# One recorded order for another: the second half of a planned fused kernel (long convolution and gated MLP, forward and backward)

## The chip, the cores and the metric

The kernel runs on one NeuronCore of a Trainium2 chip. Five instruction streams work side by side: TensorE (PE: matmuls, with PEld for its weight loads), VectorE (DVE), ScalarE (ACT), GpSimd (POOL) and SyncE (SP), which here issues all DMAs. Sixteen DMA engines move data between HBM and SBUF. Matmuls write to PSUM, eight banks of 2 KB a partition, which ACT and DVE empty. The metric is device microseconds of one launch, the median of several runs.

## What is computed

With `x = A_q` (2048 x 512) and `xn = layernorm(x)`, the output is `x + A(xn) + B(xn)`. A is a short convolution of `k` (four taps), times `v`, then a convolution over the whole sequence by FFT, plus `kv * D`, times `xn`. B is a gated product of matmuls. The program returns the output and the gradients with respect to all nine inputs:

```python
def _A_ref(q, k, v, shift_k, ssm_k, ssm_D):
    ...
    kv = k_shift * v
    ...
    y_f = kv_f * kf_f[None, :, :, :]
    y = irfft2(y_f, ...)[:, 0, :S, :]
    y = y + kv * ssm_D[None, None, :]
    return q * y
def _B_ref(x, w_gate, w_up, w_down):
    g = einsum("bsd,df->bsf", x, w_gate); u = einsum("bsd,df->bsf", x, w_up)
    return einsum("bsf,fd->bsd", g * u, w_down)
x = A_q; xn = _layernorm(x, axis=-1)
return x + _A_ref(xn, ...) + _B_ref(xn, ...)
```

## The kernel before

**How an order is set.** The program text does not fix the order of the instructions. Every call on an engine goes through the class `Eng` (L145), which only records an `Op`; matmuls that follow one another into the same PSUM slot are joined into one operation of at most 2200 columns. At the end `emit` (L181) unpacks the string `PLAN`: a list of 2271 operation numbers, and a PSUM bank for each of 398 slots. The operations are then issued in that order, so `PLAN` decides the order on PE (1009 operations), DVE (623), ACT (377), POOL (3) and SP (259 DMAs) and which buffer of PSUM each result uses. Waits between engines follow from the data: an instruction waits for what it reads, and for the readers of what it overwrites. All instructions have the line of the recording helper, L173, in the profile.

**Stages.** The first 100 us hold the loads, the layernorm, the first F steps and the short convolution (`a_gen`). The feature axis F = 1376 is cut into six F steps j. `mlp_rows(j, r)` (L417) computes for two of the sixteen row blocks the down-projected gradient `pd` and the two products `pg`, copies them out of PSUM and multiplies them; the result goes to a ring in SBUF and, through `hd_store`, to the scratch tensor HD in HBM. `dw_gen(j)` (L584) makes the weight gradients of F step j: chains of sixteen 512-wide matmuls.

The spectral stage (`s_gen`, some 125 to 257 us) takes eight pairs of slabs from scratch AX: `s_B` and `s_Bi` are packed small matmuls (tiles of 64x32 and 32x64 of the array, sixteen to an operation) with copies by ACT behind them, `s_pw` the products on DVE; the result goes to scratch CX. The stages overlap: PE alternates between `mlp_rows`, `dw_gen` and the spectral operations.

The last stage (from 268 us) runs over n = 0..7, two row blocks each:

- `c_load(n)` (L678) loads 1.5 MB of CX into the single buffer `f["C"]`; `last_dft(n)` (L721) turns it by 24 packed matmuls into three PSUM results. They are copied by ACT and used on DVE by `c_dkv`, `c_y` and `c_o5`. The next `c_load` may start only when `last_dft` has read the buffer.
- `c_dsk(n)` (L766) multiplies rows of dks by rows of k on DVE and sums them by eight packed matmuls on PE. When its products are made, `k_load(n+1)` (L693) may overwrite the rows of k. `dk_pair` (L712) is seven DVE operations and a store.
- `hd_load(n)` (L644) brings HD back transposed by DMA, into one of two buffers. `y_o(n, rr)` (L786) and `y_x(n, rr)` (L803) read it: 11 and 22 matmuls of 512 columns. `y_o` ends in an addition and a store of the output, `y_x` in a chain of DVE and ACT operations (the layernorm gradient) and a store. `y_load(n)` brings the rows of x that `c_y(n)` needs, `dkv_load(n)` two operands of `c_dkv(n)`.
- `turn_gen` (L617) transposes ring blocks of the last F steps, by DMA for some and by PE for others.

All DMAs go through SP in the recorded order. An instruction that waits on SP holds up every DMA behind it.

Of the kernel before, what the change touches and what calls it, by code (L numbers as in the profile page):

```python
# [26 lines left out]
WO = [12 * sum(SW[:j]) for j in range(NST)]  # L27
# [11 lines left out]
def kernel(  # L39
# [223 lines left out]
    XT = rT.tile("XT", [128, 16, 1024])  # L263
# [62 lines left out]
    for i in range(12):  # L326
        w = 4 if i < 4 else 2
# [254 lines left out]
    f = {}  # L582
# [251 lines left out]
    F0, F1 = 240.0, 415.0  # L834
    O0, OJ = 230.0, 10.0
# [60 lines left out]
    A = Gen(a_all())  # L896
# [42 lines left out]
    for n in range(NCH):  # L939
        last = n + 1 == NCH  # L940
        t = F0 + n * DF
# [30 lines left out]
        else:  # L972
# [115 lines left out]
```

## Time and profile before

| What | Value |
|---|---|
| Median of 3 runs | 427.74 us (427.58 to 427.88) |
| The profiled execution | 426.57 us |
| Its span, first to last instruction | 424.4 us |
| Time around the span | 2.17 us |
| PE, DVE, ACT busy | 415.1, 349.0, 261.5 us |
| Granted TensorE clock | 0.998 |
| Matmuls / DMA issues | 3290 / 259 |
| DMA moved | 127.27 MB, mean 300 GB/s |

The "busy" of PE says that a matmul was in the array; waits shorter than a matmul do not show in it. In the row of the DMA engines a digit is the mean busy share of sixteen engines in one of 40 slices of 10.6 us; in a table by stretches the same share can exceed 1, because packets that queue in an engine overlap.

### The profile page before, as it was taken

What the parts mean: (1) busy time and instruction counts of PE and PEld (TensorE: products, weight loads), DVE (VectorE), ACT (ScalarE), POOL (GpSimd) and SP (SyncE); (2) the same over time, 40 slices, a digit from 0 to 9 for tenths busy, and PEclk for the clock granted to TensorE, in tenths of its full rate; (3) what the DMA queues carried; (4) which work ended last, traced back from release to release, by engine and by line L of the source; (5) the groups of instructions that cost most, each with busy time, mean ns of one, the idle gap of its engine ahead of it and who ended that gap; (6) DMA issues with size and microseconds to landing.
All of it is one profiled execution on the core that took longest, in us unless ns stands there. A gap on an engine that the chain in (4) does not pass through costs nothing.

```text
span 424.4 us, 8338 instructions
## 1 busy us (share of the span) xinstructions
PE 415.1 (98%) x3290; PEld 209.3 (49%) x3290; DVE 349.0 (82%) x653; ACT 261.5 (62%) x380; POOL 3.5 (1%) x9
## 2 busy tenths in 40 slices
PE   8999999999999999999999999999999899999995
PEld 5755555855675444544444344445444344444443
DVE  5999977998649989899999990325858799999996
ACT  4855988598644999888999953362525331323324
POOL 1000000000000000000000000000000000000000
PEclk9999999999999999999999999999999999999999
DMA  7989999999788869968878899999999999999964
GB/s 262 398 197 379 320 306 388 349 367 365 288 310 287 319 229 352 313 227 318 319 274 344 292 312 325 298 348 274 231 275 329 303 269 329 308 302 286 267 193 144
DMA packets 104366, 127.27 MB, mean 300 GB/s; under 512 B 63876, under 2 KB 74249, under 8 KB 103304
## 3 DMA queue, kind: packets, MB, share of 16 engines
q1 hardware_dynamic: 104328, 126.75, 93.5%
q8 instruction: 25, 0.41, 0.4%
q14 instruction: 13, 0.11, 0.1%
HBM read 57.10 MB, written 54.04 MB: 262 GB/s over the span
## 4 chain that ended last, share of the span: by engine, by line
PE 77%; DMA 10%; DVE 10%; issue 1%; SPq 1%; ACTq 0%; ACT 0%
PE PP L173 77%; DVE big L173 10%; DMA out_dram<-big 4%; DMA big<-CX 2%; DMA big<-in_k_dram 2%; SPq L173 1%; DMA big<-in_w_dram 1%; DMA big<-in_go_dram 1%; ACTq L1084 0%; ACT big L173 0%
## 5 line engine op out<-in xcount | busy, mean ns | idle before, releaser
L173 PE MATMUL PP<-big 128*128 128x512 bf16 (+8 forms) x3290 | 415.1, 345 | 4.3 <-DMA big<-CX 2.1
L173 PEld LDWEIGHTS <-big 128*128 128x128 bf16 (+4 forms) x3290 | 209.3, 97 | 209.7 <-issue 61.0
L173 DVE TENSOR_TENSOR big<-big 128x1024 bf16<-128x1024 bf16 (+2 forms) x465 | 267.7, 631 | 45.5 <-ACT big L173 36.6
L173 ACT CAST big<-PP 128x512 bf16<-128x512 f32 (+2 forms) x314 | 224.4, 780 | 82.1 <-PE PP L173 71.1
L173 ACT ACTIVATE big<-big 128x1 f32<-128x1 f32 (+3 forms) x46 | 23.6, 522 | 53.4 <-DVE big L173 50.5
L173 DVE CAST big<-PP 128x512 bf16<-128x512 f32 (+1 forms) x37 | 32.4, 875 | 9.8 <-PE PP L173 5.2
L173 ACT COPY big<-PP 128x1024 bf16<-128x1024 bf16 x15 | 14.9, 1010 | 18.3 <-PE PP L173 18.3
L173 DVE SCALAR_TENSOR_TENSOR big<-big 128x512 bf16<-128x512 f32 (+2 forms) x36 | 23.3, 654 | 0.2
L173 DVE SCALAR_TENSOR_TENSOR big<-big,PP 128x512 f32<-128x512 bf16 x14 | 9.6, 684 | 9.2 <-PE PP L173 9.2
L173 DVE BATCH_NORM_STATS2 big<-big 128x6 f32<-128x512 bf16 x16 | 10.6, 682 | 4.0 <-DMA big<-in_x_dram 3.9
L173 DVE TENSOR_TENSOR big<-big,PP 128x512 bf16<-128x512 bf16 x14 | 9.2, 683 | 1.5 <-PE PP L173 1.5
L173 POOL MEMSET big<- 128x1536 bf16 (+2 forms) x3 | 2.9, 950 | 252.4 <-PE PP L173 252.4
L173 DVE TENSOR_SCALAR big<-big 128x512 bf16<-128x512 bf16 (+1 forms) x13 | 4.6, 385 | 0.0
L173 ACT ACTIVATE big<-PP 128x512 f32<-128x512 f32 x2 | 1.2, 597 | 4.5 <-PE PP L173 4.5
L173 DVE BATCH_NORM_AGGREGATE big<-big 128x2 f32<-128x6 f32 x16 | 2.3, 169 | 0.1
L173 ACT ACT_TABLE_LOAD x1 | 1.3, 1283 | 0.7 <-PEq L1076 0.7
L173 DVE RECIPROCAL big<-big 128x2 f32<-128x2 f32 (+1 forms) x9 | 1.2, 151 | 0.6 <-ACT big L173 0.6
L173 DVE DVE_READ_ACCUMULATOR big<-big 128x1 f32 x16 | 1.3, 82 | 0.0
L173 DVE DVE_READ_ACCUMULATOR big<-big,PP 128x1 f32 x14 | 1.2, 82 | 0.0
L173 DVE MEMSET big<- 128x128 bf16 (+1 forms) x2 | 0.2, 112 | 0.8 <-PEq L1076 0.8
L173 DVE COPY big<-PP 128x1024 bf16<-128x1024 bf16 x1 | 0.7, 692 | 0.2 <-PE PP L173 0.2
L173 ACT ACTIVATION_READ_ACCUMULATOR big<-PP 128x1 f32 x2 | 0.4, 194 | 0.0
(6 smaller groups left out, 0.9 us busy)
## 6 DMA issues: line engine op xcount, KB each, us to landing
HD<-big SPq DMA_DIRECT2D x32, 384.0 KB, 5.4
AX<-big SPq DMA_DIRECT2D x16, 768.0 KB, 5.6
big<-AX SPq DMA_DIRECT2D x16, 768.0 KB, 6.0
CX<-big SPq DMA_DIRECT2D x16, 768.0 KB, 5.4
out_dram<-big SPq DMA_DIRECT2D x43, 256.0 KB, 3.8
big<-CX SPq DMA_DIRECT2D x7, 1536.0 KB, 8.0
big<-in_vK_dram SPq DMA_DIRECT2D x8, 512.0 KB, 5.1
big<-in_w_dram SPq DMA_DIRECT2D x4, 768.0 KB, 7.5
```

Of the source, the lines that this page charges most:

```text
L173: o.fns.append(lambda: f(*[fix(x) for x in a], **{kk: fix(x) for kk, x in k.items()}))
```

## The change

Two things are edited. In `mlp_rows`, the matmuls of `pg` are cut into two halves of 256 columns for fewer row blocks of F step 4: those with r < 4 instead of r < 8 (that is, r = 4 and r = 6: two halves of the row pair, four matmuls each, so 16 matmuls of 512 columns take the place of 32 of 256 columns).

And `PLAN` is another string. It unpacks to the same 2271 operations, in another order from operation 1100 on, and to another bank for 145 of the 398 slots. Up to there both orders are the same. On PE the first difference is at operation 517 of 1009, which starts at 170.12 us in the trace; on SP it is DMA 112 of 259, on ACT operation 201, on DVE operation 278. POOL's order is unchanged.

```diff
-PLAN = "c-l=@V-RM$vTb+9wr$(CZQHhO+qP}nHjZbGjlseDX6~O?yDOD...
+PLAN = "c-kdb1JowD5-nH8wr$(CZQHhO+qP}nHr6w1b7t|rf8I$t-IcDJ...
...
         for rr in range(2):
             pg = rN()[:, 0:2 * fw]
-            for p in (slice(0, fw), slice(fw, 2 * fw)) if j == 3 or j == 4 and r < 8 else (slice(0, 2 * fw),):
+            for p in (slice(0, fw), slice(fw, 2 * fw)) if j == 3 or j == 4 and r < 4 else (slice(0, 2 * fw),):
                 for c in range(4):
                     MM(pg[:, p], lhsT=xnT[:, r // 2, rr, c, :], rhs=wgu(j)[:, c, p], start=(c == 0), stop=(c == 3))
```

What differs in the unpacked order of the last stage, in the places that the prediction speaks of:

- On PE `c_dsk(n)` stands directly behind a `last_dft` for n = 0 to 4 and 6, and directly ahead of one for n = 5; before, three of the eight adjoined a `last_dft`. `last_dft(4)` stands later among the other matmuls, `last_dft(5)`, `(6)` and `(7)` earlier. The last `y_x` is `y_x(7, 0)` instead of `y_x(7, 1)`, and `c_dsk(7)` stands ahead of most of the last row pair's matmuls. The last operations of PE are `y_o(7, 1)` in both.
- On SP, from the middle of the stage on: `k_load(6)`, one of `dkv_load(6)`'s two transfers and the store of `dk_pair` of rows 6 and 7 stand ahead of `c_load(6)`, the store of `y_o(4)` behind it; `k_load(4)`, `dkv_load(4)` and `y_load(3)` stand ahead of `c_load(4)`; `hd_load(1)` stands ahead of `c_load(2)`; the DMA transpose of rows 8 and 9 stands ahead of `hd_load(0)` instead of behind `hd_load(4)`; `k_load(7)` stands ahead of `hd_load(7)` and `y_load(7)` behind it. The last DMA is the store of `y_o(7, 1)` instead of that of `y_x(7, 1)`.
- On DVE the last operation is the same one, the final addition of `y_x(7, 0)`; the chain of `y_x(7, 1)` ends some operations earlier.

More of the change, by code (lines that the diff above doesn't have):

```diff
@@ L33 @@
 EPS = 1e-5
-PLAN = "c-l=@V-RM$vTb+9wr$(CZQHhO+qP}nHjZbGjlseDX6~O?yDOD+8f*2gN+$rBAPF#(fE17tia`Pp$O0uHJ|u>OfRG%DgMxuWfG7|ZqCqK$4l$rKB!iex7GgmnC<E=GBb0;K5C?KWTqq9}AQfzcc#s?BLmt=!9iS6*hSZQB3P1~J1q&c4<b^a)5V}BX$O?s^Fyw==&<(mn5vUDap&1l~me3sPLJz0|J)s^{gP|}3>O&Q%4h^6xq=QB<3}!-Os03|bB8-R1Fc=!b5U2s;pb7MXiZBg^!w9GehhaLLfmN^zn!+g910!JqtcFQ28g@fl=m%+GFZ6~LkQ2thEXaacaUbl5*{~9hz&%Keec&u4!Glm8lVS~=3v*x|B*O!62(n>KTm$`KE%b$2m>qwD$*>OA!(tc!@8w5W0s~<KEQCd{6*j{y*aqq09Q+JR;TOmNTOcD`fIlHRE`#mxE1ZWZa1nOEamWTI;67Y}9C#FdgKO{zj=^I{jwc}no`RJ4JLJU6kP2@@YWxGPgWwPFDWt))cmp25O-P4#AwA~8444rgLMFTe&ml8p#+Q&AKZ8%8Hs(RaylD6WvctdN2pF&q)<wj8*beGpeS8D?F$xyIg4h86f`<4X6vC_UITXgI*a#crTX+gZunDfirnnwA;6{80EpQY54K1-1w#GL2B{akL&=z;XHjIIzaST3zub>@9!_C+pJ79DC0y<($+=7Sk2#&{C*a<sh7wn1?up7p~qsUkbzJ^zD4F8sIpgWGm*Dx7lV-6UH|G;+ai9PT;_!g$(G@OXXaSryv>DU{$VjrA~eQ^rTz<xLh7vK(Dh%@m7?!=SWA7|kJ9EiJd5I&_LG#FRlE*ye!aUL$ip|}#4;4mDHOK~U-f-_hY=i>-`2Fr06Er(V#664`2T#T!+H7&x^*pL!pF>FM|u`wmU_}GT(({NggO{gukpk}lO8_+52OiigJoy9Ix0%y{BEQuGe6qd%0R0hvsCmKQRs4QN>L|6{5;B_Rtfj6-{UdF3f0dL`LtcbJm4vwTzbQde(LaL1SunJbii`bm*V>Nt$4{<NXqyzW}ALA2zim|9YjlyR*i(*q8ic8ONHod@?c!}cCC-^DOp+mSIKf}-Q3ye<*=u1pUiD)i;h4ZK%rJ~%FhX&I=OigL%6(*+FScdvjTDpd1X+C|8-(We)OYfuujiJkwkIGYiszAM{0DX(!;rDn2l2AHIPZcQxRidQy1OA9(DI;Z~EA$f<q@OV}C8I)=g|bp*`UQW*-!L2fj(^~vn4Jn!4*Cm|QxU2{Z}2L;#iEpx-eGSVP1ookzQ@1uA5202;(u6-ic?i8K|n}EOw~weDy%^zBd6+=k^<GB1yqxwP)W)~QK=L~qpnnoYEx;7PW9+IEv9aCgX&NZ>O)ItDQ%=>)R(%`INC(xX$Nhi0W^W0(L~x#18FTyqUW@e*3%1GN0aF#ZJ=GWg{IInnnAbdFm0x(bdXNN5!z3m&~(~Ohv-MzLkH+6t)QRi811EB=_akD-{>N(rd70@ex_gO6nzh8=u<jPpVI^SozBu4Izf-=5eff6pV31)NlzjqmD6#0X8wXQa7KPbnK(0lMPE`Deoa~VFWO4C=^mY<H<XRD^Le^MIruK+<oA?||EApR{55?`d3Y#)L-*-B%FDptQ(Q)l$1yk`8^5Jt{Emk6Z2p%<@Jx=z|H?l!lK+v4Jc?s-d>+lwISP;A0z923aRQFYGk5~W;@Dh?EAuR#!xOm*CuGxtT!<(0IIhY;_mL~;cuvHLIr58i3Mb*hT#bLA|D*^PW!9;@gsbx+D#l5<F2x{G)kPddlkrkc&e1gmN7Ds-oQiV^F3C|frY_{g97E%1O0L22v@^%mQk+UtacVBj@imRs<XT*YV`*$nt!cO{m*YW{mJ?_~EzfDSHdo-pnobjGQq9kGxC<xIx?GRbYjUm688o9d;AGmByK#3;p*^@E_v9R!NgHuv&Z)gPrN-fc+Jt*^Q*Or1IhPWQ<=onWS8-ll&Re-9XVzt$N2}^Q-p19m6&KRE+?xAv8*a<1xi44OteRc>aZz2#*>oLe(KVc3*YjHL&xN(N=F<UOMC<4)e$6Gc9hcJfTuh5=N!`wM^=sb2WweIY(w<aPOKUkTuLHRQ-{%KhLCfkxe#C>gfIjAm+L51dC2g#Oxt><hr`(B~>N9@MFZdg7qA$6!w$TRqEpOmYxRHL!ZS^y5sGsu}+)kV6cl;%{(DvF%zvmygzW&HRaR*HzNo5)j(B|4vlSvo-nOkXcNg>^IkfxN*x{*`KK<%o%beMM6;W|QhacW5;`?$BJl>@w=hj2RSslV`G{gn@Ldg-e}w59Ih-#CK|)xA7YH}hfcp<B3*j?)R6OAc`k>8BZ`zmC`Gno}}KYn`aM<#*03lXZsf<ZO~%vPd5JgNw<ZJV|G3aapbBc&+A@3v`|@@I}7FYxFXY)+<~}uJRZSGDm0WpEOT5@k|}7bM-g}E-ec*iY(HovQAI%NuICkb(C(<XtG30$TeP}8+D3K)#!4HOUg36&Nn!QEYwxHMHlNCjwze;CYP01vRpUoVZFsG^*`FCw|NCG)uZ|sALSi-hmY}H-mY(Wn#PtrT1F1(J>IKt`84m-IFe6l$Puk2NBE@Xmzr`~Ys*fJD`$C^7Lwz-TMI}$Iibh&l-|+0a#jmUe0j%(C4t=2gi=%z$!?y{@41>Jmb-dJZ)$bfuYdC`J+BA#A3mVv<hEYZfBA+!(CfNYi^yd?r{(3U{>K-zl3daXQdzF(Lj|cQt>lr`k&F7dKGtS}(psMA7y4B1Yjb&~Rpl#fAq}LFRFRhQT))xJw2d^B#`01>)z|t+UT9nSM8DH7^`88okt0t2)W`Bh>&Ywqihq;8^u9chuT|tHeJJ0m%3J+i-fMm7CQap?ey=9&#HE8gl^?Z<{H?#~ulhtfN>=$t|JC315A81hX%FcnU&+t<hy0?Q1?-iy7qXu6g+w>BUSjs8M6=%F)<ybAUx{hYBpBN#qV`<kT36{O{UwHpy^#18$D-P&62;QmOBo>X>`!?u=`6kdB?D!U43@8Dh{Up?lFEijY)fDX?Tn<cq&8E|$~j47=Owjeu*8<!F33emVi|3gT#{rqTjoe6OKG1;X1gp`<cZCd6n0hSNq);>SuL9twE2?V7RWVODA#3?<g~@|spYf6mcw${PjW*(m!g*23RoW7EqQH;d?&-@sTH@9_JfR&$97Y0Nf8?<OJ$k-EVt#2?2)oo%nI3ZSs|tEM=4>e<c^fF=Qc`8Svf0jqh+<Ml<%dgjgh@l%_`bwwomp;bsH;dWUW-N19DK-$$F__8)T!@vT-tAzL7&x(~jE&*(B}kk$o!@WwTVW$~H+ROM9ClRjh+em1(j?I$B*jEJx(1)V5C6*``Y!>tZwHSLtf?Y>_Rt7q(Tl$#yv=FYRCJX2)fRbhlrmht;=d*3%l;2{|dfY>73rowC##*<0Bqr=+npv59tCnp$t`W6i9&^|cn((pp(RYi-MHxwWxL*49?oN}Ft-+Z6l4?#fhKWz*~jn{G4gOZ&w(+bipD1MGL(Vq5J;8)&O-jcv2vY>*AMwKmg+*eM%o+ijf<v-LL1X4?)MZgcFM&9$HH6Wd@TY^Tk$UAEhPvajs5?Xi(I-!|HLTVQ+bJKJab?GGDe2W+%0wC`<<owi?XtR1v*_Qp2Zc>Bf<*#vuQhwW=SVre|Bzq5ZVsRvKz#r=kfzqcr^9^IpQ3@2yL=q21drkC_sp4cy0H2>SqSZvSaH!Y6;Y3`Tptflt?9@jH_7BA>WEvv_K^dg?bvw3BY?^mpp|7G_qyXW*Ae!*J%Rjcl$y@uEH6rR${cml8G-&%gZZ*9DT=kktT$dmbhmces-VXy6-ysUTjw%*w5_(e<T<vfo!^+cZ6>v}$~=f%9dSMVlY(W`iBPwqv%i+A;DUdh|}bnoUfyoY!9ncm*3c|UL9{e76H@&P`}C;0=b>cf46gD>)CKG;|KIv?oce5BX+hThYA`6?gfOT4c)@*&>a*ZX*1?R~ttKeTIh%SQVcZ{@dbwr}t`KEdaC3!m$2e4~%`iN47<`%B;ALw&Nh^sRo~rubez>Yw;N-{znCVxQ`t`9VM8U-(-8(&zgH-|jp7fgkgw{*|Bc1^&uk`xRg2gZ#Lk@T-2-_xLee=#TuQpYs*I+`smnzS~dvE`RKYe7|4w)BcU0_rw0JU-zee!*6;B$-^zb?ce)Ff8n1;9_4rZ7k}m{0){Bzu15`*JX*NyDZ>+|5Iwx{w;m&W=kGjCxaU9kb59jG#0<aseUBA>^t9nOfA6Wo0gn^@_H^N)OZd~%huGmK&k+9cpFMF%7@CBCJyEC_a)$r>ch?X%WDH3{(~vCu<$rj*U?EqCA1Z~)!9%7{C{zi}Lgr94WC_(m$<REM3Ry$-P%xAZ*+PxbGL#90L++406bX4ktxz<y3S~q7&^ny3HlbKZ8rp`MAwjrfcddA65b}l`p<HMe+J_QhY-kb2h1y|gC?D#F0-;+NABKeqp+o2%`h||6VW<%5guY>7=oI>gNnv<s6efqdp>tRtMuZ+=N*E9}gq~qzSQWa2O<`ad8K#9kVNjSI28XF(b(kK8gi&F0*b+`!y)ZY74qL;*uqG@Bjl=eEEo=*2!=A7x91MrT;;<tu3HieHurwSFN5Y)2EZhh?!_hD%EDy)R%y2%e4L8H_a4XCUy~2qwEA$Sx!@004TnKl<j4(g!4ZFj>a5p>)7sJVLDLfDN!u_y6tP3l`<M1H72$#c?a4I|v2f~%GGMo-C!^3bjoC#;cqkv|pk=r_O<Z{g7C?MvMmL(jS7^^#*3%ikg5EBw0LWhVa0DI()>Ks{q)JG&Tm`CEFF}X#ef7B4c2X}}(qzn<9IO2>(5k;hdM!ZZSw{uZeG=&chJhF^r2ZhKXf*MJu5i=&khzeaGVr`MGjSzukpcZkCOd?t^6puK65I4n0`2T$op^q6qfHe9@=mVXPq$~n4V)SwRXh0C51poj0p!?r$1oKC}_A!h{>Id{8Ghn2Q5#%2zMW98tKGe!17~}(H{!pO^mB>mWmHQARQlm(uh_ipFsQw?pe}w%"
@@ new lines @@
+PLAN = "c-kdb1JowD5-nH8wr$(CZQHhO+qP}nHr6w1b7t|rf8I$t-IcDJLZ2=GWPxPBPzq8(YA6ATKp-2GhJ=t55(7d?C<zJ%4gsP;bcg|EAST3uvXBB|LwSe;NuV5bgw9X_;zB&g1M#6ERDv|H84^HVSP1!G3v_}m&=t}`K_~>Rpbad7<d7fIL1E|yZ6P}pfuc|V#zPP23B{l;bcYsD99lz5s1LoM9`uF=Py>d;ENBSTpe8he>W~4NzzCQPO`!_3gUK)vs=`oc48x!nOn_$42P(r17zv}GHXMbSa1PeM9%v3@U>}TzNw5~Cz*yJ|?O_0<hyBnORzYqU2Xi1BX2%0?5az;aI0g?ODfWZ&kPHt)O-zopa6Zg~1&{&{!4b%TwQ(H`g!RxL>R?X%0j9zR*a%Bu5WJV~VHpgDO|Tf2z;@UQcVGu(gbVN^EQg;U6KsRba0z~gn79IV!q0FKrom;{1t%c~oPvjN1#;nW_yumj6F31+Atj!MRCoqb<FAk#uR<EU3u*B;xCw&a!N-se)8j381h*jr-iM5s2Qy)2d<<Fe9=wFCkQHA;Ui<_;g1VRw74xIvE654|f+JwSdRQM33t$ImfDQ3aD2UOp5EjNp_y;t`|DXt7hfkp>M#m=D6#s(fPz;;l25gQSaT9LFchCyA;NQ?1+hAL4ho3_Wd=Kq$H|)SzI2Om@Gx!2JU<}-f9kCO(#Lu8J#>Q=U6p!IVjDuaUD|W-~I0<`TJUot!b>K^Q11Ior`3idCczg>}F)rqU3HT4}#NOBozk#n|I?lk!coOGfADoGOaXa?I`Pd();Vc}0Q*aUP!o@fnPvLGnjRSEG4#L5>7l+_;8b(8L74E@d7#|nl3LK8BaT$)lk+>X((-1g^#c?5y!WXa-N6<=WL!&VPuEC|a7TeMiJd2GfF_yq4R1%v~B20+ws3DD{_1KKsQ!8pg`>+w6!LHPtTGM&#Mx}5zUBuFO3Cmzv>`dkG0(PNM)Pc(56-<H^@EYDk!drM7E8<nWj+O8Z-o?r|7w_R{8bkN73NEIq_yDV6b-au%=^@s@NB9``V{AHvPw*)|!{-=>I?@<?fpaJ>#iRK266ew@e2rHq0eyrY<2*Wo2k{g96hFg+l!!jZ#FT{Q(-*ja22dKxOZjLh9l*4dj^1EWdW+>~Af=}pSe_Qrm-rP{p#1bsI?*_~N(HDQ6{JekhYHcx_zixG*B}{Xpo~<RGEo&uPT%48IG!?77P>}1U}5?Zvr-BwLfI%gRi&TsXZ!_o(69I#{*F1RDCMF*FeMeEYV;>wr@yc`<)(Mom&Vc!I*jk}Z~O;S(ZBc~mY|YUok|f95)o4k5}FR{P|3)tCZ(o8wP+F5rf5`}@=$atLouj3)uFmnmSR!^x=Bl^2i>B2)QkGjGFncXX$AGCo-~2B&_vorJ7^G1q8BuocG6&4PgCe6?WT?NiZ;+xdQF>X4{f7qG=pZ*9Xd)|X*wOIvv7<K(nmCt_R<mhp7zlpI!>$T2RcFf>1Vo4tLYcIOlxTkt)w66Cptsl!a4ew&eEs!h<>H>w2n^EQ+h(eztJc3m`>BPh>^+}I3qKEMwvJ>zo9IgmA|0RDI33~?ED99r@QokF3_KpgLCplx<|SAKIP{3l!yPOyzKlXeNFjzIDbVC=^M(=z~54QMoz%7xBwgfMI-nfjpVufFOA~a9E1Ore`qxSBb9j!$L54QmSb`>9>;}vCQso+9Gz$JB#y&zxe8b1IXsUib2U!PriHl(Pvr?*or4}ASI~)^gp+dQ6X`Tg#znaXe@FjGF)q%m(|H-!<Rw&slXHEFMWU)pIGU#5<(!gZYATMQi})m!<WgLkqibwk%u6|z#?#bXixX&9j<01nji%wWT$U4RI<3uhxE#mPxSCeeae1!5Lnu8b(!^Sk(`#L>#7Q-SCeh?tkn3?bPNwy_0cX^d+K@A8W^KeNv^)3Uo}5a1abxbyxipJ5;ijBh`*3QF$Az^S_vPl?f?IMPB^b|nwH2@7{JN62b8F73D>$E4*9E+TYiJuTqVu^e_v3clp4W1JuBq8Irw-uax|(z72F|AIxS($2^*oS^YF#a$gSeR1(>MH<OKAr#qaC?~mekU^lk4l3yo<|eEv=)yskWBY3R+PIb0>btkGPVS*T?*Xhj1Z%%9XV<KjSLeREKf{t)|bp3pdvn{E}bsSKLfrb5(7pjr42Y#2;}J{g~V9C)`*+<<Gc-w$N|*b8e*_wTphs-*H3zo`2v@noN?*3?8H{wX>#>Zu%p)(Ug)(dgu^MEnRgpr;)+hUHj+=?WrSml<wiQl1>hAUrjHE_#hAC4ANVF;-Pw&d+9!Itr;bg9Ocp4U-$D79;SI@xK7Z#GEn>J0G*||WGiQuEHX(a>P*colXV;CkSRJ<f96%3Res@L`8Uoc7r3pi)!jT-bIL`|Cne-}Ua$FOo?fD{dWkRd7+t3&Wwy@Oaau+;>+dv27w95gs7rLbF4ir&RafX0zRE$O$u+*tH~1zm)97-Gm+CZ~u7S(SDqW)+bd#2nlU!Ps>q_0ItM!Q9=JIlyPw@^t!^e52{=t9pF1^Ed`5xcrV|s%BqlLUp_vukRt`9hd#FSVPTjEGuDJSRnfbQ0KvS0UTEjg*D^cdHX(^^|j=nOrpXL+yIl|r&z@9B9hAn~QJ6qGai7vI+eQbgYIL4Bb0rKsH2b6P|0=v}QK#pSZ@<@bC@|K=O|NQ=oAd`mBAMY*CkwWcJLM3PvN$R({LmF1#d)q2uGlFDPft}W%7R*}Pco}cJb{fGbMHd0ld>1X;-Kh^3|P1;H;`9i<a2J%)v*B9DETFY~NssAxZBWWtHw2QQtFZH#)(XX|k{I0)BW7)#rYCHKun@cl!AW!6>{HfpQclv`qlArWP?J7^@FMTZU6eSW2MMTBqd;Lg1*5~p}e%8PB7kRIp<X`<qzmQ+`7yV5?(f`z?v%HZG0@g#wK9i0T)4GcpTCf-v%X*4iFX=6Pq_41v^^^V*&k|T{%PzmkTTvSzFXT%}Z{6gTd@dO*u6-l}CB9{}K@!ap+DnOJ(JhU=mX9T^rL)AA$dcP&86rbvn4FXI@~QkTne2jGluL41u1FF~YMCvWWwEO=T&~G=$!aMql@+iXa#L=}2$?N&WUgehl$P4&$$ZIS*)5kXkcF~H7RwSTXoc+)DP%dVs4bNrB)1i_A~sT%$#PjCD`k|7mOrF~m9jkcqvW;XR?<q_D)~m9+cUc@cjT^=v(-}G?#XxZy{wV7^3*=IF)~*6$~ehq)vbn&mkBaa_DNZ*X#3@W9F#+n-)dSJt6=M7y=;(;vPmjiC97q%?WO%Go8?>iNe;^qnIw~Ciqx?!vQ?(a5?gAY*ek1I)$FJolWlTbw#yFLDJSHlos_Cp&+6J&a!R(^Hv3w3$!_^s2H9X6Vnc11Ewk;m!*<$oJ1u8qg{`zzw%Uf<2pegmY>ln8b++Di*#_Had*p<5uuXPW?#sXS!aCY$n<mp`hRl>PHrB@3c$;7oZIW%a-S(I4vAwp%I$3A?)Mm+N_MLriU978hvwhax_FE6@X|L^9t8WeLfHkyU*4r9cV{2kfZL&?VgLcRc+YvizpW9TMX47qk&9qrI+veC@n`iTFf&FMd*g{)mKiOjY!rs_#_NTqIZ|s;gv*y;qT3R3LYyGUh4X{@BrF~?rt&O#{cGlkhvfu3wduRVx3Lj|V>fhQKJ8QpKOpoQ}vHfQ|Zo#AZ6U*%9B4tl<|H{r=9FObqJiaGz_xHyBx25vbp43x%bkE{hJ)39u3wF_Rcuvpdxjmhy_Y9uV6M7ym<^Ne;kKrY~w3qR+-pM<A7w_ubyu0`Cp5EIFdNR-CiM*!g^IBfW3ws(*>&?BG*Y-MI*Xwx^FX09JlC|~3Uf+{=elO?cy@I#%rheIOSTAqoSL~{_@UN}Ccknh|)GK-eZ{(G{s#o*MUd3DbP3z+ue4}sj8eZK;ct;=Uqr9Py_ToO!2YGAX>@&QXZ}BPK*vI%#AM4|Mst@)7zSW2MHs9_${f@2nHNM2}+DxD2vwe=w_2J&%m-%vE;S+qkqhGUmzSghXI-ltCy@~hre*W4&@{fI*f8w9{LjT++IrwB><;VS)pYZ9v)Q9*NzR&mj0YB+0{f*zU^?ul&`Za&zd;OH3_P73}U-EPQ%8&R0U*wDZjPLMW{*{02-}*QH++X;0zu`Ciyx;QMzT40GBj4kfJ%kH>$M5-FzwaqSs&LR#huij@fA1Ilfj{&s{+Fi-k3Cw59%6);Ay&BRKl`8lsUPyA{><Nb?C{?I_Lu%kq>=yK|M4F@Vfe}a^`zlfPZA_(NEXtC^Z`SLkTFn*8!`nBKe~tiJVmfjIK&B=L%fhBWDVIv{7^Ym2~|V2P(9QLHAAiNhbIorLh?`~)ComH-jE=q4S7PbkS{b3EkeQ2I<yIGL%YyEbO;Zue8?7ZgxsNcC=qgoT;Y_p3?)P3&@l`T<HJ2G9V&!Qp-ZS3YKOX^UPu%Mgi_(YRSFNSe;61Vg)*UR7!gK>hT%6a6v~BGVNj?aI)|>ITNoTBgo$BP$R8$!$ze)p8hVDQp-1QyriB?{dgvXRgnnUuSP({sxnW3{7lww7VN=)~wuG%=TNoC$hcRJC7#r4vwP9CS98TLKdu%(y%&;gd35UbNur4eO%fjxkCoB)$!?>_7+z2<rt#CWs33tPaP$2XP_rim4BpeMF!>n*D91kbL%FrOJ3VXx)Fgx528^VR~FgyzTL*H;ITn>-Jldw9>2`9sqa3H)0r^3N-HJk~j!`bjOTnjJ5q3|rc3fIHAa6UW_uLDNXmqw~};7D=I;wT{I7D-=`Bx}a%&gQ~yBvI2MITMJ`A%X;8kJPBn5%R-+WJVVA$a!c?ZjsYJ><~c|93m0L5W$HfU^I$sL{e!4Wsx+jqO52NAJVdFL^>!$ekat3xCk3FMap^tREc`_DE&C1QY3Ok2?c~mNF#NQk`*B$R|I76{}Gw=L1L7WMjs4{GAGI?_^?LC2R@2ojf^O^DD6Jb76th~&_1w4I3)svNE;HtM(z^v0z_m+`o+krsP-hvDd;K^0Y+RI<soE`P#)1UisFdY645v+6i58=Kg;=r8~"
```

## The prediction

> **What bounds the kernel now.** I read the page first, then what PE waits for, then the stretches of the last stage, SP's queue, and the chain of waits.
>
> ```profile
> PE 415.1 (98%) x3290; PEld 209.3 (49%) x3290; DVE 349.0 (82%) x653; ACT 261.5 (62%) x380; POOL 3.5 (1%) x9
> ...
> DMA  7989999999788869968878899999999999999964
> ```
>
> PE is busy almost throughout, so no order can save much on PE itself. But the DMA row is 9 from slice 25 on, that is, from some 245 us, until slice 38. What PE waits for:
>
> ```profile
> PE PP L173 <- DMA big<-CX: 2.1, 2, 1.7
> PE PP L173 <- DVE big L173: 1.1, 1, 1.1
> ```
>
> The two waits for CX are for `c_load(4)` (PE resumes at 338.03) and `c_load(7)` (395.73). The stretches show how full the last stage is (columns: us, then PE, PEld, DVE, ACT, POOL busy with counts, clock, DMA share, GB/s):
>
> ```profile
> 285.00:325.00 40.00, 40.00 (x274) 19.20 (x273) 26.90 (x52) 15.60 (x21) 0.00 (x0) 1.00 1.04 277
> 325.00:365.00 40.00, 38.27 (x232) 17.10 (x234) 36.51 (x67) 10.85 (x16) 0.00 (x0) 1.00 1.12 298
> 365.00:405.00 40.00, 39.61 (x246) 17.29 (x239) 39.22 (x74) 14.14 (x20) 0.00 (x0) 1.00 1.13 293
> ```
>
> From 325 to 405 us three things are full: PE, DVE, and the DMA engines at a share above 1. An order that wants PE earlier must get its loads earlier from engines that never rest. SP's queue shows when two such loads are issued (start, length):
>
> ```profile
> 367.90 0.59 SPq L173 DMA_DIRECT2D big<-CX  x1
> ...
> 370.65 0.53 SPq L173 DMA_DIRECT2D big<-in_k_dram  x1
> ...
> 390.96 8.86 SPq L173 DMA_TRANSPOSE big<-HD  x1
> ```
>
> These are `c_load(6)`, which lands at 375.94, `k_load(6)` behind it, and `hd_load(7)`, which lands at 403.28. The end of the chain of waits:
>
> ```profile
> 387.10 8.58 DMA big<-CX
> 395.69 0.04 issue
> 395.73 23.65 PE PP L173 x143
> 419.38 0.02 issue
> 419.40 0.37 ACT big L173
> 419.77 0.72 ACTq L1084
> 420.49 0.02 issue
> 420.51 0.42 DVE big L173
> ```
>
> `c_load(7)` releases PE, PE works without a gap to 419.36, and DVE's last addition ends at 420.93. The last store is issued at 421.37; the span ends 3.05 us later, at 424.4, which is 5.06 us after PE.
>
> **PE's queue laid end to end.** Distances between starts in the trace give the price of each operation where nothing is waited for: 0.863 us for four 512-wide matmuls, 0.873 for the same work in eight halves, 0.216 for one, 0.557 for a spectral operation, 1.305 for `last_dft`, 0.548 for `c_dsk`, 0.447 for eight transposes. A change from full-array matmuls to packed ones costs 0.093 more, each time. From operation 517 (170.12 us) these sum to 241.39 us plus the changes. The old order has 43 changes: 170.12 + 241.39 + 4.00 = 415.5. The new one has 39, because `c_dsk` mostly adjoins a `last_dft`, and the halves go in four groups at 0.010 each: 170.12 + 241.39 + 3.63 - 0.04 = 415.1. So the visible edit of 16 splits is worth 0.04 us, and the saved changes 0.37.
>
> PE's real end is this sum plus the largest lateness of any operand, since a wait shifts all that follows. Old order: `c_load(7)` is wanted at 391.85 by the sum, and PE resumes at 395.73: 3.9 late, and 415.5 + 3.9 = 419.4, where the trace has 419.36. This reckoning can be carried over.
>
> **When the loads are wanted in the new order, and when they can land.** By the new sums `c_load(4)` is wanted at 337.56, `hd_load(5)` at 365.32, `c_load(6)` at 371.57 (old: 376.85), `c_load(7)` at 389.62, `hd_load(7)` at 398.39. With engines that are full, a load lands at its old landing, plus the transfers that now stand ahead of it, less those that now stand behind, less the time in which the engines had been idle. A transfer of 256 KB costs 0.89 us (262,144 B at 293 GB/s), an in-SBUF transpose 1.8 (385.05 to 386.83).
>
> - `c_load(6)`: three transfers more ahead (a `dk_pair` store, `k_load(6)`, one of `dkv_load(6)`), one fewer: 375.94 + 2 x 0.89 = 377.7.
> - `c_load(4)`: one transpose and four transfers more, less 0.3 of small ones: 337.99 + 1.8 + 3.56 - 0.3 = 343.1.
> - `hd_load(7)`: one more, one fewer: 403.3. `c_load(7)`: two fewer: 393.9.
>
> Idle time that may be won back: single microseconds in which the DMA share drops are 301 to 304 (shares 0.58, 0.36, 0.58) and 311 to 312 (0.24), together 2.2 us. They lie where SP works off the small transfers of dks in front of `hd_load(2)`, and where it waits ahead of `c_load(3)`. The new order moves those small transfers far back, so I take the 2.2 in full; the other end is nothing. After 312 there is nothing to win.
>
> Then `c_load(6)` lands at 375.5, 3.9 late; `c_load(4)` at 340.9, 3.3 late; `hd_load(7)` at 401.1, 2.7 late; `c_load(7)` at 391.7, 2.1 late. The largest is 3.9, as before: PE ends at 415.1 + 3.9 = 419.0. With nothing won back it is 6.1 and 421.2.
>
> `c_load(6)` now also stands behind a wait: `k_load(6)` must wait until DVE has multiplied the row of k that it overwrites (`c_dsk(5)`), and `c_load(6)`, `hd_load(6)` and all of SP wait behind it. By the new sums `y_x(4, 0)` leaves PE at 356.4; 3.3 late, 359.7. From there DVE has nine operations to that product, 5.4 us in their rows: 365.1. Then `c_load(6)` is issued at about 366.4, and 8.0 to the landing (as 367.90 to 375.94) gives 374.4, within the 375.5.
>
> **DVE.** For each DVE operation that PE releases I add its release by the sums to the DVE work from it to the end. Old: at most 416.2. New: at most 414.2, because `y_x(7, 1)` leaves PE earlier. With 3.9 of lateness 418.1, so DVE finishes before PE. `y_load(7)` now follows `hd_load(7)` (401.1 + 0.9 = 402.0) with 15.4 us of DVE work behind it: 417.4, also covered. If that cover goes, the old tail comes back.
>
> **The tail.** If DVE is done, the last store is that of `y_o(7, 1)`, which the old run issued 0.61 after PE's end. 0.61 + 3.05 = 3.66 instead of 5.06: 1.40 saved.
>
> **The middle, 170 to 262 us.** ACT and DVE are nearly full there (37.9 and 39.5 of 40 us in 205 to 245) and PE shows no wait. 145 slots change bank. I cannot read the cost of new bank waits from any row; the old small delays up to 268 us come to 0.8, and I bound the new ones by 0 to 2. Either is hidden, because the DMA engines, not PE, are 3.3 to 3.9 late afterwards; if that cover goes they count in full. Below nothing is excluded for the same reason.
>
> **Sum.** Span: 419.0 + 3.66 = 422.7 against 424.4, so 1.74 less. The profiled execution would be 424.8 instead of 426.57; it lies 1.17 below the median, and the same step takes the median from 427.74 to 426.0.
>
> **Where the skill speaks.** Loads land in the order of issue here: issued at 329.41, 330.04, 330.53, 331.00, landed at 337.99, 338.67, 339.35, 339.97. The Trainium skill, "DMA: Bandwidth & Descriptors", section "Queues, rings and completion order", says that completion is not FIFO per issuing engine; that is a rival below. The same page, "Measured", gives about 358 GB/s a core where both cores of a pair stream. By it, as an estimate, a 256 KB transfer costs 0.73 and the median would be 425.7; the 293 of the row decides.
>
> **Rivals.**
>
> 1. Nothing of the idle time is won back. The engines are full in both orders: speaks for it that they carry the same bytes; against it, that the dry spells have named causes which move. Lateness 6.1, span 421.2 + 3.66 = 424.9, median 428.2: no change. Chance 0.2.
> 2. Slower: SP stands at `k_load(6)`. The place is the product of `c_dsk(5)`, which in the old order is done at 370.56; DVE was full from 341 on, and the new order needs it 5.5 us sooner. If it comes at the old time, `c_load(6)` is issued at 371.8 and lands at 379.8: 8.2 late, PE ends at 423.3, span 427.0, median 430.3. It makes the kernel slower than before from a landing of 377.0 on, that is, from a product later than 367.8. For it: 39.2 of 40 us of DVE are busy; against it: the sums give 365.1. Chance 0.27.
> 3. Loads do not queue behind one another, so `c_load(6)` lands 5.2 us after its issue (its shortest service, 370.72 to 375.94), at 371.6, on time. About 1 us of lateness is left, as the small delays of the middle: 415.1 + 1 + 3.66 = 419.8, median 423.1. Against it: the landings above. Chance 0.08.
>
> **How the numbers follow.** The forecast, 426.0, has 0.45, with 424.8 to 427.0 as its own range (lateness 2.7 to 4.9); most of it, 0.42, is faster. With rival 3 that is 0.5 faster, with rival 1 0.23 the same, and 0.27 slower. A difference under 0.2% (0.86 us) cannot be told from none. The range reaches up nearly to the slow rival, and down below the forecast's own: 424.2 to 430.0.
>
> **What would show it.** Right: a PE wait for CX at `last_dft(6)`, near 374 us, as the longest; DMA share near 1 through 301 to 304; 3.7 us from PE's end to the span's. Wrong: SP standing at `k_load(6)` past 367.8; DVE ending after PE; new PE waits for ACT or DVE between 170 and 262 us, which would say that the new banks cost.

## The result, and the profile after

The changed kernel takes 431.4 us (median of 6 runs, 428.51 to 432.64) against 427.66 us before (6 runs, 426.2 to 430.36): 1.0087 times the time of the kernel before, 95% interval 1.006 to 1.0115. It is slower by 0.9%, and the time lies above the range of the prediction. Here and below, ratios and medians leave out runs that are over 1.5% above the quickest of the same kernel. The profiled execution is the quickest of the six, 428.51 us with a span of 426.7; a second profile of the same kernel (`again`, below) has a span of 430.2.

The page after: PE is busy 0.7 us less (0.4 were reckoned), and the row of the DMA engines looks as full as before.

```profile
PE 414.4 (97%) x3274; PEld 207.7 (49%) x3274; DVE 352.4 (83%) x653; ACT 261.4 (61%) x380; POOL 3.5 (1%) x9
...
DMA  8989999999698888798798999999999999999952
```

What PE waits for, after (total, times, longest):

```profile
PE PP L173 <- DMA big<-CX: 3.0, 3, 1.8
PE PP L173 <- DVE big L173: 2.2, 3, 1.1
```

The longest wait is at `last_dft(6)`: it was forecast there. The stretches of the last stage (us, PE, PEld, DVE, ACT, POOL, clock, DMA share, GB/s) show where PE lost it, from 365 us on:

```profile
325.00:365.00 40.00, 38.66 (x241) 17.80 (x239) 36.37 (x68) 13.81 (x19) 0.00 (x0) 1.00 1.08 304
365.00:405.00 40.00, 38.11 (x243) 17.30 (x245) 37.34 (x70) 11.63 (x16) 0.00 (x0) 1.00 1.07 271
```

SP's queue there: `k_load(6)`, one load of `dkv_load(6)`, then `c_load(6)`, which lands at 376.73.

```profile
366.68 0.34 SPq L173 DMA_DIRECT2D big<-in_k_dram  x1
367.07 0.48 SPq L173 DMA_DIRECT2D big<-in_vK_dram  x1
367.65 0.38 SPq L173 DMA_DIRECT2D big<-CX  x1
```

And the end of the chain of waits. PE ends at 420.57, but the chain no longer runs through PE. It runs through a store (`psd_end`'s, 4 KB), and from the landing of the store to ACT:

```profile
417.50 1.70 DMA out_dram<-big
419.24 0.04 issue
419.29 0.70 ACT big L173 x2
...
420.62 1.36 DVE big L173 x3
422.02 0.05 issue
422.07 0.81 ACT big L173
```

Laid out by the prediction's own sums, each profile has three terms: the start of operation 517 (identical work up to there, yet it differs from execution to execution), PE's lateness against its queue laid end to end, and the stretch from PE's end to the span's end.

| Profile | Operation 517 | PE late at the end | PE's end to span's end | Span |
|---|---|---|---|---|
| before | 170.12 | 3.85 | 5.06 | 424.4 |
| after | 169.33 | 6.24 | 6.17 | 426.7 |
| `again` (the same kernel) | 171.18 | 8.36 | 5.7 | 430.2 |
| forecast, at 170.12 | 170.12 | 3.9 | 3.66 | 422.7 |

PE's sum itself came out right: from its last wait, which ends at 376.78, to its end at 420.57 PE needed 43.79 us, and the prices add up to 43.56. Both other terms failed.

### The profile page after: what moved, and what is told of

Its sections match the earlier page's. It is cut to its first block, busy times and chain, and to the rows that moved or that the text cites. A ratio compares the mean times of both kernels' runs of the same rounds, so it can differ in the third digit from the quotient of the medians.

```text
span 426.7 us, 8303 instructions
## 1 busy us (share of the span) xinstructions
PE 414.4 (97%) x3274; PEld 207.7 (49%) x3274; DVE 352.4 (83%) x653; ACT 261.4 (61%) x380; POOL 3.5 (1%) x9
## 4 chain that ended last, share of the span: by engine, by line
PE 56%; DVE 20%; DMA 15%; SPq 4%; ACT 3%; issue 2%; ACTq 0%; DVEq 0%
PE PP L173 56%; DVE big L173 20%; DMA out_dram<-big 5%; DMA big<-CX 5%; SPq L173 4%; ACT big L173 3%; DMA big<-in_x_dram 2%; DMA CX<-big 1%; DMA big<-in_go_dram 1%; ACTq L1084 0%; DVEq L173 0%; ACTq L173 0%
```

## The experiments

Most edits are made where `emit` unpacks the order and only move recorded operations. `splits8` changes the splitting line, `filler` adds matmuls, and `mid_before`, `mid_after` and the kernels built on them have another `PLAN`. Ratios are against the kernel before on the same chip, with 95% intervals; medians are in us. The intervals reach 0.2 to 0.4%, 1 to 1.7 us, to either side, which is as much as most single edits win. Only those of `c0_back`, `best1`, `best2` and `best3` lie wholly below that of the changed kernel; those of `c6k_psd` and `mid_after` just touch it, and the others overlap it.

**A second profile of the changed kernel: `again`.** 

> The changed kernel unedited, for a second profile: the six runs lie between 428.5 and 432.6 and the profiled one is the fastest, so some term varies by 3 us. Theory A (PE's lateness at the CX load for n = 6 varies): PE's end less its no-wait sum is 7 to 9 us instead of 6.2, the stretch from PE's end to the span's end stays 6.1. Theory B (the tail varies): lateness 6.2, that stretch 8 to 9 us.

Measured: 431.49, 1.0099 (1.0063 to 1.0135). Lateness 8.36, tail 5.7: theory A, the lateness varies. 6.75 of it is there at 379.36, when `c_load(6)` lands; another 1.6 comes in the next 4 us without any wait, set operation by operation against the first profile. The stretches show why (columns as above; the clock is the third figure from the end):

```profile
377.00:380.00 3.00, 0.89 (x16) 0.30 (x12) 2.96 (x8) 0.00 (x0) 0.00 (x0) 0.90 1.05 256
380.00:383.00 3.00, 3.00 (x23) 0.87 (x16) 2.23 (x5) 2.52 (x4) 0.00 (x0) 0.53 1.27 290
379.41:382.82 3.41, 3.41 (x26) 1.02 (x27) 2.64 (x5) 2.34 (x4) 0.00 (x0) 0.50 1.15 258
```

PE stood 2.11 us, and then the granted clock was 0.50 for 3.41 us; in the first profile the gap was 1.82 us and the clock stayed 1.00.

**The tail: `psd_late`, `psd_late2`** (one kernel, run twice).

```diff
+        order.remove(2206); order.insert(order.index(2270), 2206)   # psd_end's store, ahead of the last DMA
```

> In the changed kernel's profile ACT stands from 416.29 to 419.29 ahead of the first operation of y_x(7, 0)'s chain, and goes on when the store of psd_end has landed. Here that one store is recorded ahead of the last DMA instead. Theory P (that store holds ACT): the operation runs at PE's result, near 417.1; DVE's idle 2.4 us behind it goes; PE's end to the span's end is 3.7 to 4.2 us instead of 6.1, and the time falls by 1.9 to 2.4 us against the changed kernel. Rival (ACT waited for PE's matmuls in truth, or DVE has as much work behind): no change, within 0.5 us.

> The kernel with psd_end's store recorded ahead of the last DMA once more, for a profile of it. Theory P: ACT's first operation of y_x(7, 0) follows PE's result with no wait for a store; DVE's idle 2.4 us there is gone; PE's end to the span's end 3.7 to 4.2 us. Against the kernel before still 2 to 3 us slower, by PE's lateness at the CX load for n = 6.

Measured: 429.03, 1.0059 (1.0038 to 1.0079), and 430.24, 1.0082 (1.0054 to 1.0109). The profiled execution of `psd_late` took 1088 us, with PE busy for 1082 of them; why is not known, and the profile read here is that of `psd_late2`. ACT's first operation of `y_x(7, 0)`, in the changed kernel and here (start, length, the idle time before it and what ended it):

```profile
419.29 0.60 ACT L173 ACTIVATE big<-PP 128x512 f32<-128x512 f32 x1 [2.99 <-DMA out_dram<-big]
```

```profile
420.55 0.60 ACT L173 ACTIVATE big<-PP 128x512 f32<-128x512 f32 x1 [0.44 <-PE PP L173]
```

The wait of 2.99 us for a store is gone and PE releases the operation. PE's end (424.87) to the span's end is 3.9 us instead of 6.2. Theory P holds, and 3.66 was a good forecast of a tail without this wait in a run whose PE ends this late; DVE is then done at 424.71. In the new order ACT's copy for `psd_end` stands ahead of this operation, in the old one behind it. The copy was done at 413.70, but SP stood until 417.06 for the store of `y_x(7, 1)`, which is recorded ahead of `psd_end`'s. By the 1.70 us that its landing took, issued at 413.70 it would have landed near 415.4, before ACT began to stand at 416.29 (an estimate). Why the operation waited for that store at all is not shown: it writes `dxn` and `s1`, the store reads `ds`, which are separate places; the wait is nevertheless set, on that store's own semaphore, as soon as the store is recorded ahead of the operation.

**The CX load for n = 6, ahead of everything: `c6_first`, `c6_psd`.**

```diff
+        order.remove(2070); order.insert(order.index(2047), 2070)   # c_load(6), ahead of dk_pair's store
```

> The load of CX for n = 6 is recorded ahead of the store of dk_pair for rows 6 and 7, so no longer behind k_load(6) and its wait for DVE (SP stood until 366.68). Theory Q (the place behind that wait costs): issued near 365.9, landing 373 to 374.5 instead of 376.7; PE's lateness there 2.5 to 4 instead of 6.0, the next wait is that of y_o(4) with 4.1; the time falls by 1.5 to 2.2 us. Rival (the DMA engines are full, so what one load gains the next ones lose): the loads for n = 7 land 1 to 2 us later, the time changes by less than 0.7 us.

> Both edits together. If the two losses are separate and in series (PE's lateness, then the tail), the gains add: 3.4 to 4.6 us below the changed kernel, about the time of the kernel before or 1 us less. If the tail hides behind an earlier PE (DVE's work sets the end), 2 to 2.5 us.

Measured: 434.25, 1.0166 (1.0127 to 1.0205), so 2.8 us slower instead of 2 faster; with the tail mended as well 430.53, 1.0091 (1.0063 to 1.0119), no different from the changed kernel. The theories of both failed. The load was issued at 370.04 and the store of `dk_pair` behind it at 370.51. DVE, in `c6_first`:

```profile
372.84 1.29 DVE L173 TENSOR_TENSOR big<-big 128x1024 bf16<-128x1024 bf16 x2
378.04 0.69 DVE L173 TENSOR_TENSOR big<-big 128x1024 bf16<-128x1024 bf16 x1 [3.92 <-DMA out_dram<-big]
```

The next `dk_pair` overwrites `f["dk"]`, of which there is one. It waits until the store has landed, 7.5 us after its issue since 1.5 MB of CX stand ahead of it, and DVE works in order. PE then waits at `last_dft(6)` for a PSUM result that DVE has not read.

**The CX load between that store and k_load(6): `c6_k`, `c6k_psd`, `c4_c6k_psd`.**

```diff
+        order.remove(2070); order.insert(order.index(2075), 2070)   # c_load(6), ahead of k_load(6)
```

> The CX load for n = 6 stands ahead of k_load(6) and the load of dkv_load(6), but still behind the store of dk_pair for rows 6 and 7. When it stood ahead of that store too, DVE's next dk_pair waited 3.9 us for the store's landing and lost more than PE won. Theory Q2 (the load's own place costs, and the store was the only thing that the other edit hurt): issued about 1 us earlier and with two transfers fewer ahead, it lands 1.8 to 2.5 us earlier, PE's gap there is under 0.5 us, the clock does not fall behind it, and the median falls by 2.5 to 4 us against the changed kernel. Rival (DVE, not the load, paces this stretch): last_dft(6) then waits for a PSUM result that DVE has yet to read, and less than 1 us is won.

> The changed kernel with the CX load for n = 6 ahead of k_load(6) (alone 1.5 to 2 us) and psd_end's store ahead of the last DMA (alone 1.2 to 2.3 us). In series, they add: 3 to 4 us below the changed kernel, 0 to 1.5 us above the kernel before. If the load for n = 4, which was 6.3 us late in that profile, sets the end now, then 2 to 2.5 us.

> As the one above, and the CX load for n = 4 also goes ahead of the three transfers that the new order set in front of it (both of dkv_load(4), y_load(3)). If that load is the next limit, PE's lateness behind it falls from 5 to 7 us to 3 to 4 and the time is 1 to 2 us below the one above, at or under the kernel before. If DVE then waits for y_load(3), as it did for 1.9 us in the kernel before, nothing is won.

Measured: `c6_k` 429.67, 1.006 (1.0034 to 1.0086), 1.7 us less than the changed kernel by the medians and 1.2 to 1.7 by the ratios, where 2.5 to 4 were expected. In its profile PE no longer waits at `last_dft(6)`; the longest wait, 2.02 us, is for the load for n = 4, which in that execution landed 2.9 us later than in the first profile, counted from operation 517. With the tail mended too, 428.22, 1.0037 (1.001 to 1.0063): 3.2 us less by the medians, 2.1 to 2.7 by the ratios. So the two losses add, as far as the intervals can tell. `c4_c6k_psd` is 429.83, 1.0073 (1.0046 to 1.0101). There the rival was right: with the load for n = 4 moved up, nothing more is won, and DVE waits 2.30 us for `y_load(3)`.

**PE's idle and the clock: `dft6_late`, `filler`.**

```diff
+        for o in (2138, 2139):                                      # dft6_late: y_o(5, 1)'s last two groups
+            order.remove(o); order.insert(order.index(2096), o)     # ahead of last_dft(6)
...
+                if i == 2096:                                       # filler: eight matmuls ahead of last_dft(6)
+                    for w in range(8):
+                        real.tensor.matmul(slots[380].base[:, 0:512], lhsT=ident[:], rhs=xn[:, 0, :], start=True, stop=True)
```

> The last two groups of y_o(5, 1), 1.5 us of full matmuls that need no CX, stand ahead of last_dft(6) instead of behind it. The load's issue and landing stay as they are. Theory R (PE stands idle some 2.1 us there, and after so long the granted clock falls to 0.7 for the next 3 us, which costs another 1.4 to 1.8 us in most runs but not in the fastest): the gap falls to 0.3 to 0.6 us, the clock stays at 1.0, the median falls by 2.5 to 3.5 us and the runs lie closer together than 428.8 to 433.7. Rival (the clock in that profile was an accident): 1.5 us, and the same spread. Rival (DVE is what lags, and gets its operands of last_dft(6) later): no gain.

> The changed kernel with eight matmuls of 512 columns added on PE ahead of last_dft(6), 1.73 us of work whose result is overwritten at once (their place is a PSUM result that last_dft(6) starts anew). They fit into the 1.8 to 2.4 us that PE waits there for CX, so nothing is delayed and nothing gained but the clock. Theory R (after 2.1 us without work the clock is granted at half for some 3 us): the clock stays at 1.0 and the mean of the runs falls by 1.0 to 1.7 us. Rival (the clock falls for another reason, or the lost time is made up by a later wait): no change within 0.5 us, or 1 us more where the load comes early.

Measured: `dft6_late` 429.83, 1.0073 (1.0045 to 1.0101), some 1.6 us less by the medians and 0.6 to 1.1 by the ratios, no more than the moved work alone gives, with a gap of 0.55 us and the clock at 1.00. `filler` 431.39, 1.0118 (1.0084 to 1.0152): nothing gained. Its profile shows the clock kept at full pace through the same place:

```profile
377.00:380.00 3.00, 2.11 (x26) 0.98 (x27) 2.81 (x6) 0.32 (x1) 0.00 (x0) 1.00 1.18 188
380.00:383.00 3.00, 3.00 (x24) 1.19 (x14) 2.24 (x4) 2.93 (x6) 0.00 (x0) 1.00 1.27 290
```

So half of theory R is borne out: the idle and the clock go together. That this costs a further 1.0 to 1.7 us in the whole is not shown; in the profile that has it, it costs 1.6 us of PE's time at that place, and the series with the matmuls in the gap is no quicker.

**The splits: `splits8`** (`r < 8` put back, order as changed). 

> The 16 splits alone are put back (two halves of 256 for r < 8 instead of r < 4), the order stays. They were reckoned at 0.04 us of PE. Expected within 0.5 us of the changed kernel. Rival (a result of 1024 in two halves lets ACT begin earlier, and the banks of the middle stage come free sooner): 0.8 us faster or more.

Measured: 431.2, 1.0094 (1.0061 to 1.0127). No difference from the changed kernel can be told.

**Which half of the order costs: `mid_before`, `mid_after`.** `PLAN` is a third string here. The order in it is one plan's first 1694 or 1695 operations, then all others in the order of the other plan, so for `mid_before`:

```python
first[:1694] + [i for i in second if i not in set(first[:1694])]
```

> The first 1694 operations in the order and banks of the kernel before (to about 272 us, so the whole spectral stage), the rest in the order and banks of the changed one. Theory E (the last stage's order costs it all): within 0.8 us of the changed kernel, some 4 us above the one before. Theory M (the middle's new banks and order make PE wait for ACT, 1.4 to 2.7 us late at 253 us against 0.8, and this is handed on to the end): 1 to 2 us below the changed kernel.

> The other half: the first 1695 operations as in the changed kernel, the rest as in the kernel before (seven PSUM results of the seam take another bank). Theory E: within 0.8 us of the kernel before. Theory M: 1 to 2 us above it. If both halves cost less than the whole does, they are no sum: what is late in the middle is what makes the end's loads late.

Measured: old middle and new end 429.59, 1.0064 (1.0041 to 1.0087); new middle and old end 428.22, 1.0044 (1.0027 to 1.0062). 0.64% and 0.44% add up to 1.08%, about the whole (0.87 and 0.99% in the two series). Theory E fails: with the old end behind it the middle costs 0.44%, and that is not hidden. Whether it is by the mechanism that theory M names is asked next.

**What of the middle: `turn_back`, `c0_back`** (both edits in `mid_after`).

```diff
+        order.remove(1723); order.insert(order.index(1969) + 1, 1723)   # turn_back: the transposing DMA
...
+        for o in (1752, 1754):                                          # c0_back: two quarters of c_load(0),
+            order.remove(o); order.insert(order.index(1586) + 1, o)     # behind the stores of s_Bi(6, 2)
```

> The kernel with the changed middle and the old end (1.4 to 1.9 us above the kernel before), and in it the DMA transpose of rows 8 and 9 goes back to behind hd_load(4). Theory T (this transpose, ahead of hd_load(0) and c_load(1), makes the CX loads 1.8 us later, down to that for n = 4): 1 to 1.9 us faster, about the time of the kernel before. Theory B (the new banks make PE wait for ACT at 252 us and after): within 0.5 us of the one without this edit.

> The kernel with the changed middle and the old end (1.4 to 1.9 us above the kernel before), and in it two of the four quarters of the first CX load go back to behind the stores of s_Bi(6, 2). Theory S (they delay that store, its landing holds ACT, and ACT holds PE): the store lands some 2 us earlier, ACT no longer waits for it by more than 0.5 us, PE's lateness at 254 us is under 1 us, and the time falls by 1 to 1.9 us, to within 0.8 us of the kernel before. Rival (the lateness at 254 us is hidden by later waits, and the middle costs elsewhere): ACT's wait goes, the time stays within 0.5 us.

Measured: 429.42, 1.0063 (1.0038 to 1.0089), and 428.99, 1.004 (1.0022 to 1.0059): neither gains anything. `c0_back` did what was meant at its place. ACT's copy for `s_Bi(7, 1)` in `mid_after`, and in `c0_back`:

```profile
249.66 1.01 ACT L173 CAST big<-PP 128x1024 bf16<-128x1024 f32 x1 [1.68 <-DMA CX<-big]
```

```profile
251.94 1.01 ACT L173 CAST big<-PP 128x1024 bf16<-128x1024 f32 x1 [1.42 <-PE PP L173]
```

The wait for the store became one for PE, as in the kernel before, and PE has no wait at 252 to 254 us; yet the time stays, so the rival is right. PE's wait there is small and varies: it is missing in the profile of `mid_after` too, 0.3 us in the first profile of the changed kernel, 0.8 in `again`, 1.4 in `turn_back`. Counted from operation 517, the last quarter of `c_load(0)` lands at 97.07 in the kernel before and at 97.04 in `mid_before`, but at 99.60 in `mid_after`, 99.37 in `turn_back` and 99.33 in `c0_back`; the load for n = 4 lands at 167.86 before and at 169.74, 170.29 and 169.21. With either of the two edits the first load is still 2.3 us late. That each of the two causes is enough by itself would explain it; no run has both, and what of the middle costs stays open.

**All mended places together: `best1`, `best2`, `best3`.** `best1` is `mid_before` with the edits of `c6_k` and `psd_late`, `best2` adds that of `dft6_late`, `best3` is the changed kernel with these three and that of `c0_back`.

> The old middle, the new end, and in it the CX load for n = 6 ahead of k_load(6) and psd_end's store ahead of the last DMA. The old middle gained 1.6 us, these two together 3 us: if the losses are separate, 4.3 to 4.9 us below the changed kernel, and within 1 us of the kernel before on either side. If something else of the new end is late then (hd_load(7), DVE behind y_load(7)), 1 to 2 us above it.

> As best1, and the last two groups of y_o(5, 1) ahead of last_dft(6). Where the load for n = 6 comes in time already, this only moves 1.5 us of work: within 0.5 us of best1. Where it still comes late in some runs, 0.5 to 1 us faster, with less spread.

> The changed kernel with four places mended: those two quarters, the CX load for n = 6 ahead of k_load(6), the last two groups of y_o(5, 1) ahead of last_dft(6), and psd_end's store ahead of the last DMA. If these are the whole loss, it runs like best2 (old middle with the last three), within 0.8 us of the kernel before, 4 to 5 us below the changed one. If more of the middle costs, 1 to 2 us above best2.

Measured: 427.51, 1.0019 (0.9997 to 1.0041); 426.77, 1.0005 (0.9985 to 1.0025); 427.99, 1.0012 (0.9987 to 1.0037). All three run like the kernel before, none beats it. With the old middle, the two places of `c6_k` and `psd_late` account for the whole difference; that of `dft6_late` adds nothing that can be told. `best3` keeps the new middle but for two quarters of `c_load(0)`, an edit that won nothing in `mid_after`, its first load comes as late as in the changed kernel (99.60), and still it runs like the other two. So behind the mended end no cost of the middle can be told (the interval reaches to 0.37%), and whether the 0.44% is there at all with the new end is not shown.

The mended kernels end on DVE. In `best2` it stands for `y_load(7)` and then works without a gap to the end:

```profile
406.44 0.69 DVE L173 TENSOR_TENSOR big<-big 128x1024 bf16<-128x1024 bf16 x1 [1.44 <-DMA big<-in_x_dram]
```

From PE's end to the span's end it is 4.70 us there, 5.26 in `c6k_psd` (a wait of 2.23 for the same load), 4.71 in `best1` and 4.25 in `best3`, not the 3.9 of `psd_late2`.

## Why the prediction was wrong, point by point

- **PE's sum and the splits: right.** Over the last 44 us the prices are 0.2 short; `splits8` shows that the visible edit is worth nothing that can be told.
- **The tail: the step that failed first.** "If DVE is done, the last store is that of y_o(7, 1)" gave 1.40 saved. DVE was not done: ACT had stood 2.99 us for the landing of `psd_end`'s store, DVE stood 2.36 us behind it, and the tail grew by 1.1 in the profile. Without this wait it is 3.9, near the forecast. The step reckoned what releases operations by data; it never asked what each store, by landing, holds back. By the two series of `psd_late` this is worth 1.2 to 2.5 us by the medians, 0.2 to 1.7 by the ratios. A second condition of the step, which counts once PE comes earlier, failed as well: "`y_load(7)` now follows `hd_load(7)` (401.1 + 0.9 = 402.0) ... also covered". Counted from operation 517 that load was forecast at 231.9 and landed at 235.1 in the first profile and at 236.8 in `best2`, and "the old tail comes back" in part.
- **The lateness at `c_load(6)`: the right place, the wrong size.** `c_load(4)` came as forecast: the dry spell at 301 to 304 us filled up (shares 0.86, 1.60, 1.05), and counted from operation 517 it landed at 170.86 where 170.8 was forecast. (Of the four transfers that now stand ahead of it, the one listed as `k_load(4)` is `k_load(3)`.) `c_load(6)` landed at 207.40 and in `again` at 208.14, where 205.4 was forecast. The step that failed is "From there DVE has nine operations to that product, 5.4 us in their rows: 365.1", and with it the 8.0 us from issue to landing. `y_x(4, 0)` left PE at 359.10, counted so 0.2 later than forecast, but DVE took it up only at 360.78:

```profile
358.63 2.23 DVE L173 TENSOR_TENSOR big<-big 128x1024 bf16<-128x1024 bf16 x4 [1.25 <-DMA out_dram<-big]
360.78 0.68 DVE L173 SCALAR_TENSOR_TENSOR big<-big,PP 128x512 f32<-128x512 bf16 x1
```

  DVE stood for the landing of the store of `y_x(2)`, which reads the buffer that the next `c_y` overwrites, and then had four operations ahead of the one that I started from; the nine took 5.9 us. The product was done at 366.66, counted so 2.35 later than forecast, SP stood until then, and the load took 9.1 us instead of 8.0 with two transfers just ahead of it. This is the place of the slow rival and half its mechanism: the product came just ahead of the rival's tipping point (197.3 where 197.7 is the limit, counted so), and only the longer load carried the landing past 206.9. `c6_k` shows 1.2 to 1.7 us for it.
- **The middle: "Either is hidden" failed with the old end, and stays open with the new one.** It costs 0.44% by `mid_after`. PE's new waits for ACT at 252 us, which I had named as the sign to look for, are there, but nothing shows that they are the cost: `c0_back` has none and gained nothing. The first CX loads land 2.3 to 2.5 us later and the load for n = 4 lands 1.4 to 2.4 later; that the one is handed on to the other is not shown, and in `best3` the first load is as late and the time is that of the kernel before.
- **The range.** It ended at 430.0, short of the slow rival's own 430.3. The load and the tail were treated as if one of them at most could go wrong; they are in series, both did, and their losses add.

Rival 1, nothing won back, has the right lateness in the first profile (6.1 forecast, 6.24 measured), but by luck: the dry spells did fill. Rival 3, loads that do not queue, found no support: the store that was put behind a 1.5 MB load in `c6_first` landed 7.5 us after its issue. The Trainium skill, "Perfetto Trace Analysis", section "DMA Instruction — HWDGE (DVE, Sync)", says that a DMA's semaphore rises only when the write before it is confirmed, and that this can take surprisingly long when HBM is written. The runs here agree in direction: the landing of a store of 4 KB came 1.70 us after its start with only stores about it (417.50), and that of one behind a load 7.5.

## What to carry to other kernels

When an order is changed, list for each store which later instruction overwrites what it reads, and reckon the store's landing like that of a load: with one buffer it holds a whole in-order engine, and every transfer that is moved ahead of the store adds to that hold. An engine that is full is not released by the operation in front of it alone, so start its chain from the work queued on it, not from the other engine's end. Where small losses lie in series along one path, add them; do not give each a chance of its own as if only one could happen. And ask what the next limit is: here DVE, behind a late load, took back part of what the mended places gave.

## What the runs showed of the hardware

After 2.11, 2.25 and 2.40 us without a matmul (`again`, `psd_late2`, `mid_before`) the granted clock fell to 0.50 for 3.41 us, beginning at 379.41, 380.20 and 377.85, 0.05 to 1.05 us after the matmuls went on. It fell so as well in `c6_psd`, after gaps of 0.98 and 1.73 us close together, and in `c6_first`, for 6.83 us, beginning within the second of two gaps of 1.04 and 1.73; after 1.82 (after) and 2.02 (`c6_k`) it stayed 1.00. The idle time has packed matmuls on one or both sides, and no run tells whether those count as idle. The Trainium skill, "TensorE: Matmul & The Clock Gate", section "What's actually happening", has the array at half its clock after an idle window of about 3.4 us that runs freely; the half agrees with 0.50, and the 3.41 us for which it lasted with the length of that window; the gaps here were shorter than it.

One program's runs lie 3 to 5 us apart (428.76 to 433.7 in `again`, 425.22 to 428.57 for the kernel before in the same series); operation 517, behind identical work, starts between 169.2 and 172.5 us in the profiles. A difference of 1 us therefore needs a series, and a single profile may be the quickest of it.
